# Weights of 64 bits cut to 32: raw words that land two bytes further, one cast and one join

## The chip, the cores and the metric

The kernel runs on one core of one Trainium2 chip. The metric is the device time of one execution in microseconds (us); smaller is better. The engines of the core are PE (TensorE: the matrix engine), DVE (VectorE), ACT (ScalarE), POOL (GpSimd) and SP (SyncE), which issues nearly all the DMAs.

## What is computed

Attention over 4 batches, 8 heads, 768 positions and 64 columns a head, in which a query sees the first n_global keys and the n_local keys up to itself, with a slope for each head; then two layers of two products each over 3072 tokens, with `h cos(h)` and `relu(h)` squared between them. q, k and v are 32-bit; the four weight matrices come in as 64-bit floats.

```python
def _moe_ref(x, w_in, w_out):            # 3072 x 512, 512 x 2048, 2048 x 512
    h = x @ w_in
    g = h * np.cos(h)
    return (g @ w_out).astype(np.float32)

def _moe2_ref(x, w_in, w_out):
    h = np.maximum(x @ w_in, 0.0)
    return (h * h @ w_out).astype(np.float32)

def reference(...):
    attn_out = _attn_ref(q, k, v, n_global, n_local)
    x = attn_out.transpose(0, 2, 1, 3).reshape(B * S, H * D)
    return _moe2_ref(x=_moe_ref(x=x, ...), ...)
```

## The kernel before

The 3072 tokens are cut into 24 tiles of 128 and six blocks of four tiles. Products run in 16-bit floats: each operand is split into a high half and what is left of it (a cast on ScalarE, then a subtraction on VectorE or GpSimd, `split_lo`, line 471, all recorded under line 474), and three products of halves are summed in PSUM. Only the attention of the first block (`group32`, line 762) runs in 32-bit products, since its operands then need no splitting. For each pair of heads and tile it goes: bias and scores on PE (lines 871 and 788), the maximum and its scaling on VectorE (lines 878 and 882), the exponential on ScalarE (line 886), a scaled unit matrix on VectorE (line 803), a transposing product (line 816), a copy (line 821), the product with the values (line 831), a copy into x (line 840). The other blocks' attention is `group` (line 891).

Weights come as 64-bit words. `decoded` (line 554) makes 32-bit floats of two tiles, 1024 words in each of 128 partitions: a DMA of 1024 KB (line 558) brings the raw words into a `raw` tile; ScalarE scales the upper words' absolute value, read as floats (`magnitude`, line 56); VectorE shifts it up by three bits (line 62), puts in the three top bits of the lower word (line 65), and puts in the sign (line 68), in place, in a `dec` tile. `weight` (line 566) then splits `dec` into 16-bit halves. The 16 decodes of the first layer lie at the beginning, up to the end of the first block's first layer; the 16 of the second layer come later (`seven_weights`, line 633, and `second_weights`, line 1551).

The instructions of the fast path are laid out by `Plan` (line 149). Each piece of work has an engine or several that may take it, an estimated duration, a due time, and the buffers that it reads and writes. The plan runs a model of the five engines, takes the ready piece with the earliest due time on each, gives out buffer slots, and writes the instructions down in the order found. Each engine executes its list in order. The `SHIFTS` table (line 84) moves the due times of groups of pieces: ('A', tile, pair) attention, ('P', tile) the loads and splits of a tile, ('W', e, unit) first-layer weights (e = 0: w_in, e = 1: w_out), ('X', tile) what follows a tile. The products of the two layers (`pe`, line 1110) keep the order in which they are written. Where the model finds PE idle before 240 us, filler matmuls on a tile of zeros are put in (line 1755).

Two raw slots, two dec slots and nine `ld` slots (used for keys, values and split weights) are shared by all. A DMA that waits for a slot stands at the head of SP's queue, with all later ones behind it. The slow, general path (line 1797) is not executed with these inputs.

Of the kernel before, what the change touches and what calls it, by code (L numbers as in the profile page):

```python
# [51 lines left out]
W_MAG = 2.0 ** -111  # L52


def magnitude(nc, t, r):
    nc.scalar.activation(out=t.bitcast(FP32), in_=r[:, :, 1].bitcast(FP32), func=ACTF.Abs, scale=W_MAG)


def join_steps(nc, t, r):

    return (
        lambda: nc.vector.tensor_scalar(  # L62
            out=t, in0=t, scalar1=3, scalar2=None, op0=ALU.logical_shift_left
        ),
        lambda: nc.vector.scalar_tensor_tensor(  # L65
            out=t, in0=r[:, :, 0], scalar=29, in1=t, op0=ALU.logical_shift_right, op1=ALU.bitwise_or
        ),
        lambda: nc.vector.scalar_tensor_tensor(  # L68
            out=t, in0=r[:, :, 1], scalar=-0x80000000, in1=t, op0=ALU.bitwise_and, op1=ALU.bitwise_or
        ),  # L70
    )

# [12 lines left out]
    ('A', 0, 0): 7.9,  # L85
    ('A', 0, 1): -2.2,
    ('A', 1, 0): -4.4,
    ('A', 1, 1): -2.2,
    ('A', 2, 0): -2.2,
    ('A', 2, 1): -2.2,  # L90
    ('A', 3, 0): -2.2,
    ('A', 3, 1): -2.2,
    ('A', 4, 0): -2.2,
    ('A', 4, 1): 4.2,
    ('A', 5, 0): -2.2,
    ('A', 5, 1): -19.1,
    ('A', 6, 0): -2.2,
    ('A', 6, 1): -2.2,
    ('A', 7, 0): -6.5,
    ('A', 7, 1): -8.6,  # L100
    ('A', 8, 0): -2.2,
    ('A', 8, 1): -2.2,
    ('A', 9, 0): -2.2,
    ('A', 9, 1): 1.7,
    ('P', 1): -1.8,
    ('P', 2): 7.8,
    ('P', 4): -21.4,
    ('P', 6): 9.8,
    ('P', 9): -13.4,
# [8 lines left out]
    ('W', 1, 0): -18.2,  # L118
    ('W', 1, 1): -12.2,
    ('W', 1, 2): -18.2,  # L120
    ('W', 1, 3): -13.1,
    ('W', 1, 4): -18.2,
    ('W', 1, 5): -12.7,
    ('W', 1, 6): -18.2,
    ('W', 1, 7): -24.7,
    ('X', 7): -17.9,
    ('X', 8): 3.7,
}
EARLY = 30.0
ROUNDS = 1  # L130
# [294 lines left out]
def fast_path(ctx, tc, kq, vt, w, n_raw, out, judge, ask):  # L425
# [39 lines left out]
    def new(pool):  # L465
        return Buf(pool)

    def lo_ways(n=512):
        return (("DVE", (n + 151) / 960, True), ("POOL", (n * 2.6 + 100) / 1200, True))
# [1327 lines left out]
def general_path(ctx, tc, kq, vt, w, raw, x_d, out):  # L1797
# [101 lines left out]
    def weights(m, e, j):  # L1899
# [4 lines left out]
        for f in join_steps(nc, t, r):  # L1904
            f()
# [102 lines left out]
```

## Time and profile before

| | us |
|---|---|
| median of 3 runs (lowest, highest) | 1084.62 (1083.74, 1085.63) |
| the profiled execution | 1085.72 |
| its span, first to last instruction | 1084.0 |
| PE busy | 1060.6 (98%) |
| DVE busy | 802.8 (74%) |
| ACT busy | 752.9 (69%) |
| POOL busy | 245.1 (23%) |

Busy times are those of the whole span; stages have different limits, so the rows below cut the span into stretches. The first matmul of the first layer begins at 61 us, and the last of its 16 first-layer weight pairs are decoded after 141 us. Matmuls are pipelined, and the ends of their records are modelled, so a busy PE need not be PE at its peak; filler matmuls count as busy.

### The profile page before, as it was taken

What the parts mean: (1) busy time and instruction counts of PE and PEld (TensorE: products, weight loads), DVE (VectorE), ACT (ScalarE), POOL (GpSimd) and SP (SyncE); (2) the same over time, 40 slices, a digit from 0 to 9 for tenths busy, and PEclk for the clock granted to TensorE, in tenths of its full rate; (3) what the DMA queues carried; (4) which work ended last, traced back from release to release, by engine and by line L of the source; (5) the groups of instructions that cost most, each with busy time, mean ns of one, the idle gap of its engine ahead of it and who ended that gap; (6) DMA issues with size and microseconds to landing.
All of it is one profiled execution on the core that took longest, in us unless ns stands there. A gap on an engine that the chain in (4) does not pass through costs nothing.

```text
span 1084.0 us, 23236 instructions
## 1 busy us (share of the span) xinstructions
PE 1060.6 (98%) x9380; PEld 753.3 (69%) x9380; DVE 802.8 (74%) x1483; ACT 752.9 (69%) x1349; POOL 245.1 (23%) x192
## 2 busy tenths in 40 slices
PE   6999999999999999999999999999999999999997
PEld 5754545554454444666666689888888888888887
DVE  7999997558688796677886687788368568477364
ACT  6999868998887674765876896555377457267361
POOL 1123320111140220233261221223024223033010
PEclk9999999999999999999999999999999999999999
DMA  6498888847867794778789897787564333334201
GB/s 234 171 243 250 238 282 246 152 97 238 229 177 209 295 338 157 246 226 229 249 272 261 233 232 222 268 315 255 195 216 135 127 137 127 128 117 156 86 4 41
DMA packets 160687, 217.69 MB, mean 201 GB/s; under 512 B 110464, under 2 KB 110976, under 8 KB 159040
## 3 DMA queue, kind: packets, MB, share of 16 engines
q1 hardware_dynamic: 160576, 216.17, 65.0%
q8 instruction: 74, 1.21, 0.5%
q14 instruction: 37, 0.30, 0.1%
HBM read 153.23 MB, written 36.70 MB: 175 GB/s over the span
## 4 chain that ended last, share of the span: by engine, by line
PE 83%; DVE 11%; ACT 4%; issue 1%; DMA 0%; DVEq 0%; SPq 0%; ACTq 0%
PE hps L1232 25%; PE ypps L1141 14%; PE hps L1125 13%; PE ypps L1368 11%; PE ypps L1438 7%; PE ypps L1183 7%; PE hps L922 2%; PE hps L983 2%; PE hps L1368 2%; DVE dec L65 1%; DVE nm L878 1%; DVE dec L68 1%; DVE dec L62 1%; DVE t L1426 1%; DVE xy L474 1%
## 5 line engine op out<-in xcount | busy, mean ns | idle before, releaser
L1232 PEld LDWEIGHTS <-ld 128*128 128x128 f16 x2400 | 234.0, 98 | 35.3 <-issue 2.6
L1232 PE MATMUL hps<-ys,ld 128*128 128x256 f16 x1680 | 195.1, 273 | 1.8 <-DVE t L1426 1.8
L1141 PE MATMUL ypps<-g,ld 128*128 128x512 f16 x768 | 177.8, 382 | 1.6 <-DVE g L474 1.6
L1125 PE MATMUL hps<-xy,w 128*128 128x512 f16 x768 | 174.5, 379 | 0.0
L1426 DVE TENSOR_TENSOR t<-hps,t 128x512 f32<-128x512 f32 x160 | 110.0, 688 | 66.4 <-PE hps L1232 64.3
L1141 PEld LDWEIGHTS <-ld 128*128 128x128 f16 x768 | 74.3, 98 | 90.2 <-issue 2.7
L1125 PEld LDWEIGHTS <-w 128*128 128x128 f16 x768 | 73.9, 98 | 86.2
L474 DVE TENSOR_TENSOR g<-t,g 128x512 f16<-128x512 f32 (+1 forms) x128 | 101.0, 793 | 26.0 <-ACT g L1209 25.2
L1209 ACT ACTIVATE g<-t 128x512 f16<-128x512 f32 x128 | 79.3, 622 | 23.5 <-DVE t L1165 21.8
L1183 PE MATMUL ypps<-g,ld 128*128 128x256 f16 x768 | 89.2, 273 | 0.5 <-DVE g L474 0.5
L1438 PE MATMUL ypps<-ld,g 128*128 128x512 f16 x384 | 89.5, 379 | 0.0
L1183 PEld LDWEIGHTS <-ld 128*128 128x128 f16 x768 | 75.0, 98 | 9.4 <-issue 0.6
L1423 ACT ACTIVATE t<-t 128x512 f32<-128x512 f32 x72 | 45.0, 624 | 48.9 <-DVE t L1426 48.6
L474 POOL TENSOR_TENSOR g<-t,g 128x512 f16<-128x512 f32 (+1 forms) x24 | 30.8, 1284 | 195.0 <-ACT g L1209 185.1
L1165 DVE SCALAR_TENSOR_TENSOR t<-t,hps 128x512 f32<-128x512 f32 x72 | 48.9, 682 | 31.9 <-ACT t L1163 31.9
L1161 ACT ACTIVATE t<-hps 128x512 f32<-128x512 f32 x72 | 42.7, 592 | 34.0 <-PE hps L1125 25.4
L1438 PEld LDWEIGHTS <-g 128*128 128x128 f16 x384 | 36.7, 98 | 37.1
L1163 ACT ACTIVATE t<-t 128x512 f32<-128x512 f32 x96 | 60.4, 629 | 2.6
L1258 ACT ACTIVATE t<-t 128x512 f32<-128x512 f32 x96 | 60.3, 628 | 2.5
L954 ACT ACTIVATE e<-e,nm 128x256 f32<-128x256 f32 (+1 forms) x128 | 52.7, 482 | 8.3 <-DVE nm L946 8.1
L946 DVE CUSTOM_DVE_ANT_0 e<-hps,bias 128x256 f32<-128x256 f32 (+2 forms) x128 | 43.2, 395 | 18.0 <-PE hps L922 17.9
L631 POOL TENSOR_TENSOR t<-t 128x256 f32<-128x256 f32 x18 | 16.4, 909 | 158.0 <-DVE x L631 157.9
(228 smaller groups left out, 1943.6 us busy)
## 6 DMA issues: line engine op xcount, KB each, us to landing
ld<-w SPq DMA_DIRECT2D x154, 512.0 KB, 4.3
raw<-w SPq DMA_DIRECT2D x32, 1024.0 KB, 6.6
w<-ld SPq DMA_DIRECT2D x44, 512.0 KB, 3.6
ld<-kq SPq DMA_DIRECT2D x23, 512.0 KB, 6.0
ld<-vt SPq DMA_DIRECT2D x24, 256.0 KB, 5.3
yd<-xy SPq DMA_DIRECT2D x6, 1024.0 KB, 5.8
xy<-yd SPq DMA_DIRECT2D x6, 1024.0 KB, 6.6
ld<-w SPq DMA_DIRECT2D x24, 256.0 KB, 4.0
```

The lines of the kernel that those rows point to most:

```text
L474: op.emit = lambda: eng[op.eng].tensor_tensor(out=out_f(), in0=src_f(), in1=hi_f(), op=ALU.subtract)
L954: nc.scalar.activation(out=at(e)[:, x, 0:W], in_=at(e)[:, x, 0:W], func=ACTF.Exp, bias=at(nm)[:, x:x + 1], scale=-1.0,)
L1125: nc.tensor.matmul(out=at(ps), lhsT=w_view(wt)[:, a, j % 2, k * 128:(k + 1) * 128], rhs=x_view(src)[:, c, k, :], start=(n == 0), stop=(n = ...
L1141: nc.tensor.matmul(out=at(y_ps[d]), lhsT=wv[:, a, d * 128:(d + 1) * 128], rhs=at(g)[:, c], start=(j == 0 and n == 0), stop=(j == NJ - 1 an ...
L1163: act(due + 1.2, 512, lambda: nc.scalar.activation(out=at(t), in_=at(t), func=ACTF.Square, scale=HALF_TURN), w=[t])
L1183: nc.tensor.matmul(out=at(y_ps[d])[:, 256 * n:256 * n + 256], lhsT=w_view(wt)[:, a, u, d * 128:(d + 1) * 128], rhs=at(g)[:, z, 256 * u:256 ...
L1209: act(due, 512, lambda: nc.scalar.activation(out=at(g)[:, 0], in_=at(t), func=ACTF.Copy), r=[t], new=[g])
L1232: nc.tensor.matmul(out=at(bank)[:, 256 * u:256 * u + 256], lhsT=wv(a, u, kk), rhs=sv(c, kk), start=(fresh and u == n == 0), stop=(last and ...
L1258: act(due, 512, lambda: nc.scalar.activation(out=at(t), in_=at(t), func=ACTF.Square), w=[t])
L1368: nc.tensor.matmul(out=at(bank)[:, 256 * half:256 * half + 256], lhsT=gv(home)[:, z, c0:c0 + 128], rhs=wv(a, u), start=(q == half == u == ...
L1426: dve(due, 0.7, lambda: nc.vector.tensor_tensor(out=at(t), in0=at(bank), in1=at(u), op=ALU.add), port=False, **k)
L1438: nc.tensor.matmul(out=at(y_ps[d]), lhsT=at(g)[:, z, 256 * u + d % 2 * 128:256 * u + d % 2 * 128 + 128], rhs=wv[:, a, u], start=(q == i == ...
```

## The change

A raw tile gets two more words a partition, and the DMA writes its data beginning two bytes into the row. A 32-bit word read at odd places then holds the upper half of the low word and the lower half of the high word, and shifted right by 13 it gives 19 bits of the wanted word. The topmost half-word of the 64-bit word, read as a bfloat16, is cast to float16 by ScalarE with a scale of 2, into the upper half of a word of a `top` tile whose lower halves were set to zero once. One VectorE instruction shifts and ors the two into a fresh `dec` tile. There is one `top` slot, and the cast's target is held until the join has read it.

Besides: in `group32` the scores come first and the bias is added after them, as a piece of its own; the scaling of the maximum is a piece of its own that VectorE, GpSimd or ScalarE may take; the bias tiles of the heads are built in another order, and two casts of the global tokens come after them; the cast of n stands later in `build_bias`; the 32-bit unit matrix is gone (the 16-bit one is read, and copied once near the end); the plan's model counts GpSimd's steps and the DMA rate otherwise and begins at 1.3 us; the `SHIFTS` are others.

```diff
-W_MAG = 2.0 ** -111
-def magnitude(nc, t, r):
-    nc.scalar.activation(out=t.bitcast(FP32), in_=r[:, :, 1].bitcast(FP32), func=ACTF.Abs, scale=W_MAG)
-def join_steps(nc, t, r):
-    return (
-        lambda: nc.vector.tensor_scalar(
-            out=t, in0=t, scalar1=3, scalar2=None, op0=ALU.logical_shift_left
-        ),
-        lambda: nc.vector.scalar_tensor_tensor(
-            out=t, in0=r[:, :, 0], scalar=29, in1=t, op0=ALU.logical_shift_right, op1=ALU.bitwise_or
-        ),
-        lambda: nc.vector.scalar_tensor_tensor(
-            out=t, in0=r[:, :, 1], scalar=-0x80000000, in1=t, op0=ALU.bitwise_and, op1=ALU.bitwise_or
-        ),
-    )
+UP = S_W ** 0.125
+def shifted(r, n):
+    return r.bitcast(INT16)[:, 1:4 * n + 1]
+def top_half(nc, t, r, n):
+    nc.scalar.activation(
+        out=t.bitcast(FP16).rearrange("p (c b) -> p c b", b=2)[:, :, 1],
+        in_=r.bitcast(BF16)[:, 4:4 * n + 4].rearrange("p (c b) -> p c b", b=4)[:, :, 0], func=ACTF.Copy, scale=UP)
+def join(nc, f, t, r, n):
+    nc.vector.scalar_tensor_tensor(
+        out=f, in0=r[:, 0:2 * n].rearrange("p (c b) -> p c b", b=2)[:, :, 1], scalar=13, in1=t,
+        op0=ALU.logical_shift_right, op1=ALU.bitwise_or)
...
 SHIFTS = {
-    ('A', 0, 0): 7.9,
-    ('A', 0, 1): -2.2,
-    ('A', 1, 0): -4.4,
+    ('A', 0, 0): -4.4,
+    ('A', 0, 1): 24.0,
+    ('A', 1, 0): -13.6,
...
-    ('P', 2): 7.8,
-    ('P', 4): -21.4,
+    ('P', 2): 33.0,
+    ('P', 4): -28.2,
...
-    ('W', 0, 0): -18.2,
-    ('W', 0, 1): -18.2,
-    ('W', 0, 2): -30.9,
-    ('W', 0, 3): -19.4,
-    ('W', 0, 4): -16.1,
-    ('W', 0, 5): -18.2,
-    ('W', 0, 6): -18.2,
-    ('W', 0, 7): -18.2,
+    ('W', 0, 0): 3.9,
+    ('W', 0, 1): -8.0,
+    ('W', 0, 2): -15.2,
+    ('W', 0, 3): -8.5,
+    ('W', 0, 4): -20.3,
+    ('W', 0, 5): -10.8,
+    ('W', 0, 6): -11.3,
+    ('W', 0, 7): -11.3,
...
+BEGIN = 1.3
+RATE = 320.0
...
-        raw=(2, [128, 1024, 2], INT32), ld=(9, [128, 1024], FP32), ...
+        top=(1, [128, 1024], INT32), raw=(2, [128, 2050], INT32), ld=(9, [128, 1024], FP32), ...
...
-        nc.vector.tensor_copy(out=ident32, in_=ident)
...
-        nc.vector.tensor_copy(out=nf, in_=n_raw[:, :, 0])
...
         nc.vector.tensor_tensor(out=t, in0=t, in1=rel, op=ALU.add)
+        nc.vector.tensor_copy(out=nf, in_=n_raw[:, :, 0])
...
+        nc.gpsimd.memset(slots["top"][0], 0)
...
     def decoded(m, e, jj, due):
-        t, raw = new("dec"), new("raw")
+        f, t, raw = new("dec"), new("top"), new("raw")
         dma(due - 12, 1024, lambda: nc.sync.dma_start(
-            out=r().rearrange("p (u a) b -> p u (a b)", u=2),
-            in_=w[m, e, 2 * jj:2 * jj + 2].bitcast(INT32).rearrange("u p c -> p u c")), new=[raw])
-        act(due - 7, 1140, lambda: magnitude(nc, at(t), r()), r=[raw], new=[t])
-        for n, us in enumerate((0.69, 1.22, 1.22)):
-            dve(due - 5.6 + 1.3 * n, us, lambda n=n: join_steps(nc, at(t), r())[n](), r=[raw] if n else [], w=[t])
+            out=shifted(at(raw), 1024).rearrange("p (u c) -> p u c", u=2),
+            in_=w[m, e, 2 * jj:2 * jj + 2].bitcast(INT16).rearrange("u p c -> p u c")), new=[raw])
+        act(due - 7, 1024, lambda: top_half(nc, at(t), at(raw), 1024), r=[raw], new=[t])
+        dve(due - 5.6, 1.22, lambda: join(nc, at(f), at(t), at(raw), 1024), r=[t, raw], new=[f])
...
-        plan.add((("PE", 2.0, False),), s, scores, r=reads, new=ps, lag=0.3, after=[biased[h] for h in heads])
+        k = dict(part=reads) if T == g == 0 else dict(r=reads)
+        plan.add((("PE", 1.3 if t else 0.65, False),), s, scores, new=ps, lag=0.3, **k)
+        plan.add((("PE", 0.65, False),), s + 0.5, lambda: add_bias(ps, g, adds, last=True), w=ps, lag=0.3,
+                 after=[biased[h] for h in heads])
         dve(s + 1, 1.4 * W / 256, lambda: largest(ps, nm, W), port=False, r=ps, new=[nm])
+        scaled(nm, s + 2.5)
...
+    def scaled(nm, due):
+        o = plan.add((("DVE", 0.17, True), ("POOL", 0.2, True), ("ACT", 0.21, False)), due, None, w=[nm])
...
-    dist_of = dve(0.0, 4.0, build_bias, r=[], after=())
-    for h in range(H):
-        biased.append(act(4.0 + PAIR * (h // 2), 320, lambda h=h: head_bias(h), after=[dist_of]))
+    dist_of = dve(0.0, 5.4, build_bias, r=[], after=())
+    biased = {}
+    for n, h in enumerate((0, 1, 4, 5, 2, 3, 6, 7)):
+        biased[h] = act(4.0 + PAIR * (n // 2), 215, lambda h=h: head_bias(h), after=[dist_of])
```

## Rows read from the trace of the kernel before

**Rows 1.** Stretches: bounds, length, PE, PEld, DVE, ACT, POOL busy, granted clock, DMA, GB/s.

```profile
0.00:20.00 20.00, 10.17 (x66) 7.53 (x67) 12.43 (x31) 12.60 (x32) 3.46 (x20) 1.00 0.85 302
20.00:61.00 41.00, 39.99 (x467) 30.60 (x467) 40.20 (x64) 37.70 (x93) 5.70 (x3) 1.00 0.53 160
61.00:141.00 80.00, 77.34 (x610) 39.22 (x609) 75.08 (x96) 71.61 (x114) 26.08 (x16) 0.99 0.87 247
141.00:161.00 20.00, 20.00 (x145) 9.38 (x145) 19.30 (x26) 11.35 (x18) 4.67 (x3) 0.94 0.79 274
161.00:1060.00 899.00, 894.74 (x7940) 650.35 (x7933) 647.85 (x1253) 617.38 (x1088) 205.17 (x153) 1.00 0.65 199
```

**Rows 2.** Stretches, instructions of line 1755 alone: length, PE and PEld busy, then as before.

```profile
20.00:61.00 41.00, 5.87 (x25) 2.21 (x25) 1.00 0.53 160
61.00:141.00 80.00, 2.06 (x8) 0.60 (x7) 0.99 0.87 247
```

**Rows 3.** Waits of PE over the span: us in total, times, longest us.

```profile
PE hps L871 <- ACT bias L523: 8.0, 2, 7.2
PE ypps L1141 <- DVE g L474: 1.6, 1, 1.6
```

**Rows 4.** Timeline of DVE and POOL near 133 us: start, us, instruction, idle time before.

```profile
133.48 3.15 DVE L65 SCALAR_TENSOR_TENSOR dec<-raw,dec 128x1024 int32<-128x1024 int32 x1
...
133.41 2.13 POOL L474 TENSOR_TENSOR ld<-dec,ld 128x1024 f16<-128x1024 f32 x1 [4.24 <-ACT ld L571]
```

**Rows 5.** The page's chain that ended last, share of the span by engine.

```profile
PE 83%; DVE 11%; ACT 4%; issue 1%; DMA 0%; DVEq 0%; SPq 0%; ACTq 0%
```

**Rows 6.** Instructions by source line: ns lowest/median/highest, first and last start, form.

```profile
L56 ACT ACTIVATE dec<-raw x32: 1125/1142/1220, 16.3 to 457.2; 128x1024 f32<-128x1024 f32 x32
...
L62 DVE TENSOR_SCALAR dec<-dec x32: 674/686/2089, 18.3 to 458.5; 128x1024 int32<-128x1024 int32 x32
...
L65 DVE SCALAR_TENSOR_TENSOR dec<-raw,dec x32: 1205/1224/3146, 19.1 to 464.9; 128x1024 int32<-128x1024 int32 x32
...
L68 DVE SCALAR_TENSOR_TENSOR dec<-raw,dec x32: 1211/1222/3153, 23.4 to 466.2; 128x1024 int32<-128x1024 int32 x32
...
L571 ACT ACTIVATE w<-dec x8: 1040/1044/1121, 27.4 to 138.9; 128x1024 f16<-128x1024 f32 x8
```

**Rows 7.** Stretches, DVE busy in line 62 (first two), line 68 (last two).

```profile
0.00:61.00 61.00, 3.43 (x5) 1.00 0.63 207
61.00:141.00 80.00, 8.54 (x9) 0.99 0.87 247
...
0.00:61.00 61.00, 6.09 (x5) 1.00 0.63 207
61.00:141.00 80.00, 10.98 (x9) 0.99 0.87 247
```

**Rows 8.** DMA issues: tiles, times, KB each, median us from issue to landing.

```profile
raw<-w SPq DMA_DIRECT2D x32, 1024.0 KB, 6.6
...
ld<-kq SPq DMA_DIRECT2D x2, 256.0 KB, 4.7
```

**Rows 9.** Waits of SP's queue from 0 to 145 us.

```profile
SPq L558 <- DVE dec L68: 41.3, 9, 10.7
```

**Rows 10.** Timeline of SP, DVE, ACT and PE in the first 12 us.

```profile
1.38 0.69 SPq L742 DMA_DIRECT2D ld<-kq  x1
...
3.51 0.17 DVE L504 CAST nf<-n_raw 128x2 f32<-128x2 int32 x1 [1.65 <-DMA n_raw<-n]
...
11.52 1.28 DVE L878 TENSOR_REDUCE nm<-hps 128x2 f32<-128x512 f32 x2
...
6.30 2.98 ACT L523 ACTIVATE bias<-dist 128x320 bf16<-128x320 f32 x8 [0.44 <-DVE dist L519]
...
9.13 0.80 PE L788 MATMUL hps<-ld 64*128 64x128 f32 x4
```

**Rows 11.** Timeline of PE near 61 us.

```profile
61.05 2.75 PE L1125 MATMUL hps<-xy,w 128*128 128x512 f16 x12
```

More of the change, by code (lines that the diff above doesn't have):

```diff
@@ L429, in fast_path @@
     kinds = dict(
[L430 removed]
+        top=(1, [128, 1024], INT32), raw=(2, [128, 2050], INT32), ld=(9, [128, 1024], FP32), ys=(4, [128, 2048], FP16), kq=(3, [128, 2, 2, HR, 128], FP16),
         v=(3, [128, H * (D + 1)], FP32), kg=(1, [128, 2, HR, GLOB], FP16), vg=(1, [GLOB, 2, H, D + 1], FP16),
@@ L485, in dve, with dma @@
         return plan.add((("DVE", us, port),), due, fn, **k)
-    def dma(due, kb, fn, issue=0.45, rate=300.0, **k):
+    def dma(due, kb, fn, issue=0.45, rate=RATE, **k):
         return plan.add((("SP", (issue, kb / rate), False),), due, fn, **k)
@@ L747, in prepare32 @@
             src = lambda: f4(f)[:, 0, :, 0:GLOB]
-            act(s + 30, 128, lambda: nc.scalar.activation(out=at(kg)[:, 0], in_=src(), func=ACTF.Copy), r=[f], new=[kg])
+            done = [biased[7]]
+            act(s + 30, 128, lambda: nc.scalar.activation(out=at(kg)[:, 0], in_=src(), func=ACTF.Copy), r=[f], new=[kg], after=done)
             dve(s + 31, 0.3, lambda: nc.vector.tensor_tensor(
@@ L753, in prepare32 @@
             act(s + 30, 512, lambda: nc.scalar.activation(
-                out=at(vg)[:, 0, :, 0:D], in_=hv(), func=ACTF.Copy, scale=S_V), r=[vf], new=[vg])
+                out=at(vg)[:, 0, :, 0:D], in_=hv(), func=ACTF.Copy, scale=S_V), r=[vf], new=[vg], after=done)
             dve(s + 31, 0.7, lambda: nc.vector.scalar_tensor_tensor(
@@ L872, in add_bias @@
                     out=p[:, :, c0:c1], lhsT=ident, rhs=bias[:, h0:h0 + 2, b0:b0 + c1 - c0],
-                    start=(n == 0), stop=False, skip_group_check=True,
+                    start=(n == 0 and not last), stop=last, skip_group_check=True,
                 )
@@ L1586, in farthest @@
             measured.append(last)
-        ps = new("h")
+        ps, unit = new("h"), new("t")
         def turned():
             for i in range(2):
-                nc.tensor.matmul(out=at(ps)[0:1, 128 * i:128 * i + 128], lhsT=longest[:, i:i + 1], rhs=ident32,
+                nc.tensor.matmul(out=at(ps)[0:1, 128 * i:128 * i + 128], lhsT=longest[:, i:i + 1], rhs=at(unit)[:, 0:128],
                                  start=True, stop=True)
-        plan.add((("PE", 0.5, False),), due + 1, turned, new=[ps], lag=0.3, after=measured)
+        dve(due, 0.3, lambda: nc.vector.tensor_copy(out=at(unit)[:, 0:128], in_=ident), new=[unit])
+        plan.add((("PE", 0.5, False),), due + 1, turned, r=[unit], new=[ps], lag=0.3, after=measured)
         def bound():
@@ L1730, in idle_products @@
                 continue
-            if last is not None and o.start < SPIN_UNTIL and biased[0].end < o.start:
+            if last is not None and o.start < SPIN_UNTIL and biased[7].end < o.start:
                 gap = o.start - last.end
@@ L1897, in general_path @@
                 )
+    top = gc.tile([128, 512], INT32, name="g_top")
+    vec.memset(top, 0)
     def weights(m, e, j):
-        r = gw.tile([128, 512, 2], INT32, tag="raw", name="g_raw")
-        nc.sync.dma_start(out=r.rearrange("p a b -> p (a b)"), in_=w[m, e, j].bitcast(INT32))
+        r = gw.tile([128, 1026], INT32, tag="raw", name="g_raw")
+        nc.sync.dma_start(out=shifted(r, 512), in_=w[m, e, j].bitcast(INT16))
         t = gw.tile([128, 512], INT32, tag="w", name="g_w")
-        magnitude(nc, t, r)
-        for f in join_steps(nc, t, r):
-            f()
+        top_half(nc, top, r, 512)
+        join(nc, t, top, r, 512)
         return t.bitcast(FP32)
```

98 lines of the change are left out of this document (53 added, 45 removed).

## Prediction

> **What bounds the kernel now.** I read three views in this order: busy time by stretch, what the matrix engine (PE) waits for, and the chain that ended last. The stretches [rows 1] show three regimes. From 161 to 1060 us PE is busy 894.74 of 899 us: nothing that makes another engine lighter can give more than the 4.3 us that are missing there. Between 20 and 61 us (attention of the first four tiles, 32-bit products) VectorE is the fullest engine, 40.20 of 41 us; PE shows 39.99, but 5.87 of that is filler matmuls of line 1755 that only keep it awake [rows 2], so its real work is 34.1 us. Between 61 and 141 us (first block of layer 1, while its weights are decoded) PE has 77.34 of 80 busy, 2.06 of it filler, VectorE 75.08, ScalarE 71.61: three engines near full together. The waits of PE agree [rows 3]: 8.0 us in two waits for the bias tiles at the very beginning, and 1.6 us for a VectorE result. That one is at 138 to 140 us [rows 4]: a join of line 65 met a GpSimd step that began at 133.41 us, took 3.15 us instead of 1.22, and the results PE needed stood behind it. After the stall the granted clock is 0.94 over 141 to 161 us [rows 1]: part of that stretch ran at 1.2 GHz instead of 2.4, worth 0.06 x 20 = 1.2 us. The chain puts 83% of the span on PE and 11% on VectorE [rows 5], and that 11% is the first 140 us.
>
> So the question is how much of PE's missing time before 161 us the change gives back. It is at most: 20 - 10.17 = 9.8 us in 0 to 20 us (most of it the loads' arrival), 41 - 34.1 = 6.9 in 20 to 61, 2.66 + 2.06 = 4.7 in 61 to 141, 1.2 after.
>
> **The change part by part.**
>
> *Decode.* Before, a pair of weight tiles costs one ScalarE pass (1.14 us) and three VectorE passes (0.69 + 1.22 + 1.22 = 3.13 us) [rows 6]. After, one ScalarE cast and one VectorE shift-and-or with the same two int32 inputs and the same strides as line 65, so 1.22 us. Removed from VectorE: 1.91 us for each of 32 decodes, 61 us in all, but 16 of them belong to layer 2, where PE is full: those give nothing. In the time that counts the lines that go (62 and 68) had 3.43 + 6.09 = 9.5 us before 61 us, and 8.54 + 10.98 = 19.5 us between 61 and 141 [rows 7]; line 62 there takes 0.95 us a time instead of 0.69, since it too meets GpSimd. VectorE therefore drops from 40.2 to about 31 of 41 us, and from 75 to about 56 of 80. It stops being the bound. What is next is ScalarE in 20 to 61 us (37.70 of 41) and PE itself, closely followed by ScalarE (71.61), in 61 to 141.
>
> *The ScalarE cast* reads half-words 8 bytes apart and writes half-words 4 bytes apart; the trace of before has no such pass. The nearest rows are line 56 (words 8 bytes apart, 1.14 us) and line 571 (dense words to half-words, 1.04) [rows 6]. I take 1.14, so ScalarE is unchanged; the other end is 0.1 us less for each of the 14 to 16 decodes before 161 us, some 1.5 us. A loss is not excluded if half-word writes with gaps are slower: at twice line 56, the nine decodes of 61 to 141 us would cost ScalarE 10 us, more than the 8.4 it has idle there. I keep that end for rival two. The Trainium skill (ScalarE: Activation LUTs, What ACT_TABLE_LOAD costs) gives an activation with immediate scale 186 ns + 0.833 ns an element for fp32 and bf16 alike, 1.04 us here as an estimate; line 56, at 1.14 us, shows that the stride is not free. By the page ScalarE would end 1.5 us lighter and the sum below at most 1 us lower.
>
> *The landing.* A raw tile of 1024 KB lands 6.6 us after its issue [rows 8] and DMA is busy 0.87 of 61 to 141 us at 247 GB/s [rows 1], 19.8 MB, of which the nine or ten raw tiles are about half (10 x 1.05 = 10.5 MB). What two bytes of offset cost no row shows. Lower bound 0; upper bound, each packet twice as long. I take 0 because the runs stay 4096 bytes long, and price the other end as a rival. The Trainium skill speaks against the change here (DMA: Bandwidth & Descriptors, How a descriptor splits into AXI transactions): a descriptor that does not begin on a 256-byte boundary takes one more transaction. For 4096 bytes that is 17 for 16, an estimate of 6%, and would move the share from 0.87 to 0.90, which changes no term; no run here shows it yet.
>
> *Buffers and the load queue.* A raw slot is freed by the single join instead of by the third pass, and the output slot is taken only at the join. SP's queue stood 41.3 us in nine waits of line 558 for line 68 [rows 9], with the later loads queued behind; these waits shrink. Against that, the cast's target "top" has one slot: the next cast waits for the last join, and ScalarE's later work stands behind it. A decode's turn is then about 1.14 + 1.22 us plus hand-overs, against one decode in about 9 us, so I cost it at nothing; the cover is gone when a join meets GpSimd (rival three).
>
> *The beginning.* PE's first products waited 7.2 us for the bias [rows 3], the first score products ran at 9.13, the first maximum began at 11.52 [rows 10]. Now scores go first and need only half of the first load (issued at 1.38 us; a 256 KB half takes 4.7 [rows 8], so 6.1 us); the bias tiles of the four heads of the first group come first of eight rather than among six (8 in 2.98 us, so 0.75 us less), and the cast that waits for n (3.51 us) stands two VectorE steps later, 0.8 us less. First group complete about 7.5 us, its maximum some 3.5 us earlier. Bounds 1 to 4; I take 3.0. The two global-token casts moved behind the eight bias tiles come back as two short casts on ScalarE, which is 7.4 us idle in 0 to 20 us. A bias product that waits at PE's head holds the next group's scores, as before. The zeroing of "top" falls to GpSimd, idle 16.5 of 20 us. All at nothing.
>
> *Shifts.* Of the first-layer weights, the w_in units come due later (seven of eight, by 7 to 22 us), the w_out units within 6 us of before, so fewer decodes press between 20 and 61 us. Tile 2's loads come due 25 us later, tile 4's 7 us earlier; all pass through one SP queue, in which a load that has no free slot holds those behind. I cost this inside the terms. The new scaling step (any of three engines), the unit-matrix copy near the end and the 16-bit unit matrix in line 803 are single short steps in stretches where VectorE now has room: nothing.
>
> **Sum**, against the profiled execution (1085.72 us, span 1084.0): beginning 3.0; 20 to 61 us 2.0 (between 0 and the 6.9 of PE; ScalarE allows 41 - 37.7 = 3.3, and hand-overs keep part); 61 to 141 us 2.7 of 4.7; the clock 1.2; after 161 us 0. Together 8.9, so 1076.8 us. The median of the runs is 1084.62, 1.1 lower than the profiled one, so 1075.7.
>
> **The rivals.**
>
> 1. *PE bound from the start.* All covers work: 4 + 6.9 + 4.7 + 1.2 and half of the 4.3 us after 161 us, 19 us: 1066. For it: VectorE's relief is far larger than the holes. Against: ScalarE at 37.7 of 41.
>
> 2. *ScalarE takes VectorE's place.* It loses nothing by the change and is 92% and 90% full. Then only the beginning and the clock are won, 4.2 us: 1080.4.
>
> 3. *The single slot and GpSimd.* A join that meets a GpSimd step takes 3.15 us; the next cast waits, and behind it on ScalarE the sine and the halves that PE needs. The stall at 138 us cost 1.6 us and 1.2 by the clock, 2.8 together. Three more like it cancel the gain, four or five make it slower: 1084 to 1088. Against: VectorE is no longer full, so there is less to stand behind.
>
> 4. *The landing at two bytes is slow (slower than before).* With raw tiles x longer, DMA's share of 61 to 141 us is 0.87 (1 + 0.53 x). It decides from x = 0.28 (share 1); from x = 0.45 the overrun eats the gain; with x = 1 the share is 1.33, 26 us over: 1105.
>
> **How the numbers follow.** Forecast (1071 to 1079.5) 0.53; rival one 0.13; two 0.16; three 0.11 (half unchanged, half slower); four 0.07. The range takes in rivals one and two and half of three: 1066 to 1085. A difference of 0.2% (2.2 us) is about what a measurement of this kernel can tell from none. Faster 0.82, within 0.2% 0.05, slower 0.13.
>
> **What would show it.** Right: VectorE about 31 of the stretch that now is 20 to 61 us, the first matmul of line 1125 some 5 us before 61.05 us [rows 11], fewer fillers, no clock below full after 30 us, the rest of the span as long as before. Wrong: raw tiles landing much later than 6.6 us, the cast over 1.2 us, waits of PE for ScalarE in the first block, or new waits after 161 us where I put zero.

## The result, and the profile after

| | before, us | after, us |
|---|---|---|
| median (lowest, highest) | 1084.18 (1083.63, 1085.63) | 1068.97 (1068.91, 1069.69) |
| the profiled execution | 1085.72 | 1068.98 |
| its span | 1084.0 | 1067.3 |

After over before is 0.9859, with an interval of 0.9842 to 0.9876: 15.2 us less, where 8.9 were forecast. The column of before is of the runs that shared the chip with after; its median is 0.4 us below the one that stands ahead of the prediction.

The stretches of the profile after, with the columns of [rows 1] (length, PE, PEld, DVE, ACT, POOL, granted clock, DMA share, GB/s), then the filler matmuls of two of them alone, which answer to [rows 2]:

```profile
0.00:20.00 20.00, 12.88 (x106) 10.14 (x107) 14.66 (x29) 14.21 (x44) 5.10 (x21) 1.00 0.88 328
20.00:61.00 41.00, 40.16 (x482) 30.80 (x482) 31.48 (x50) 40.75 (x97) 8.92 (x4) 1.00 0.66 189
61.00:141.00 80.00, 79.70 (x625) 40.00 (x624) 63.68 (x85) 76.94 (x122) 23.35 (x14) 1.00 0.88 265
141.00:161.00 20.00, 20.00 (x183) 11.12 (x181) 14.58 (x32) 19.23 (x29) 0.00 (x0) 1.00 0.92 274
161.00:1060.00 899.00, 897.47 (x7961) 657.31 (x7960) 615.21 (x1229) 612.43 (x1076) 185.23 (x137) 1.00 0.64 196
...
20.00:61.00 41.00, 2.98 (x13) 1.19 (x13) 1.00 0.66 189
61.00:141.00 80.00, 0.82 (x3) 0.21 (x3) 1.00 0.88 265
```

VectorE is no longer the full engine: 31.48 of 41 us instead of 40.20, 63.68 of 80 instead of 75.08. ScalarE is: 40.75 of 41 and 76.94 of 80. PE without its fillers does 37.18 us of work between 20 and 61 us (34.12 before) and 78.88 between 61 and 141 (75.28 before), and the granted clock is 1.00 from 20 us on, so the dip to 0.94 after 141 us is gone. VectorE would have been at about 56 of 80 us by the prediction. It is at 63.68 because 11 joins fall into that stretch instead of nine decodes, and because it now takes 11 of the subtractions for `g` there (9.2 us) instead of five (4.4), and five of those for the weights (8.0 us) instead of two (2.4).

What PE waits for over the span (us in total, times, longest), against [rows 3]; the page's chain that ended last, against [rows 5]; and three lines of the timeline, of PE, of VectorE and of PE again, against [rows 10, 11]:

```profile
PE hps L791 <- DMA ld<-kq: 5.4, 2, 4.5
PE hps L1250 <- DVE t L1444: 1.3, 1, 1.3
PE hps L890 <- ACT bias L530: 1.2, 2, 0.8
...
PE 92%; ACT 5%; DVE 2%; DMA 0%; issue 0%; SPq 0%; DVEq 0%; ACTq 0%
...
4.54 1.23 PE L791 MATMUL hps<-ld 64*128 64x128 f32 x8 [4.54 <-DMA ld<-kq]
...
6.99 0.42 DVE L897 TENSOR_REDUCE nm<-hps 128x2 f32<-128x256 f32 x1 [1.32 <-PE hps L890]
...
53.72 2.75 PE L1143 MATMUL hps<-xy,w 128*128 128x512 f16 x12
```

The bias tiles cost PE 1.2 us instead of 8.0; what it waits for first is now the load. In the chain the 11% of VectorE have become 2% and ScalarE has 5%. The first maximum begins 4.5 us earlier (6.99 against 11.52) and the first matmul of the first layer 7.3 us earlier (53.72 against 61.05).

The clock column says 1.00 for the first 20 us of both kernels, but the matmuls themselves say otherwise. The same product of 128x128 32-bit values (line 816, now 823), in before from 19 to 20.5 us and in after around 14 us (ns lowest/median/highest, first and last start):

```profile
L816 PE MATMUL ypps<-t,e x4: 411/421/580, 19.5 to 20.3; 128*128 128x128 f32 x4
```

```profile
L823 PE MATMUL ypps<-t,e x8: 275/275/420, 13.5 to 14.4; 128*128 128x128 f32 x8
```

In before these products begin 0.21 us apart until 20.5 us and 0.11 us apart from 20.7 us on, and last 275 ns then too. That is a factor of two, as between the two levels of the clock. So PE comes to its full speed some 7 us earlier in after, at 13.7 instead of 20.6 us. That is about what the first layer gains; how much of the gain is its doing, no run shows.

Since the products of the two layers have the same order in both kernels, the n-th matmul of a line can be set against the n-th of before. (Up to some 205 us attention products lie between them in other places, and the difference moves up and down by some us.) That gives the place of the gain: 7.3 us at the first matmul of the first layer, 12.5 from some 205 us of before on, 12.9 at 430 us, 16.6 at the end. I call 12.9 the early part and 3.7 the late part; every experiment below has the same two numbers, from its own profiled execution against that of before. That execution of before is 1.5 us above the median of 1084.18, so the two numbers add up to 1.4 us more than the 15.2 of the medians.

The decode, as [rows 6] had it (ns lowest/median/highest, first and last start, form), and the landing of the raw tiles, as [rows 8]:

```profile
L62 ACT ACTIVATE top<-raw x32: 1338/1352/1447, 19.9 to 425.1; 128x1024 f16<-128x1024 bf16 x32
L69 DVE SCALAR_TENSOR_TENSOR dec<-raw,top x32: 1206/1224/1261, 21.7 to 427.2; 128x1024 int32<-128x1024 int32 x32
...
raw<-w SPq DMA_DIRECT2D x32, 1024.0 KB, 6.1
```

The join costs 1.224 us as forecast, and GpSimd never holds it up: six of the 32 overlap a GpSimd step in time, but the longest takes 1.261. The cast costs 1.352 us; I took 1.14. The raw tiles land no later than before.

### The profile page after: what moved, and what is told of

Read it like the earlier page. It is cut to its first block, busy times and chain, and to the rows that moved or that the text cites. A ratio compares the mean times of both kernels' runs of the same rounds, so it can differ in the third digit from the quotient of the medians.

```text
span 1067.3 us, 23170 instructions
## 1 busy us (share of the span) xinstructions
PE 1052.0 (99%) x9364; PEld 750.8 (70%) x9364; DVE 741.9 (70%) x1426; ACT 763.6 (72%) x1363; POOL 222.6 (21%) x176
## 4 chain that ended last, share of the span: by engine, by line
PE 92%; ACT 5%; DVE 2%; DMA 0%; issue 0%; SPq 0%; DVEq 0%; ACTq 0%
PE hps L1250 27%; PE ypps L1159 15%; PE hps L1143 14%; PE ypps L1386 12%; PE ypps L1201 8%; PE ypps L1456 8%; PE hps L1002 2%; PE hps L940 2%; PE hps L1386 2%; ACT e L904 1%; ACT top L62 1%; PE hps L791 1%; ACT t L828 1%; DMA ld<-kq 0%; PE hps L1586 0%
## 5 line engine op out<-in xcount | busy, mean ns | idle before, releaser
L480 DVE TENSOR_TENSOR g<-t,g 128x512 f16<-128x512 f32 x131 | 98.6, 755 | 28.6 <-ACT g L1227 28.1
L1441 ACT ACTIVATE t<-t 128x512 f32<-128x512 f32 x72 | 45.0, 625 | 50.9 <-DVE t L1444 50.6
L480 POOL TENSOR_TENSOR g<-t,g 128x512 f16<-128x512 f32 (+1 forms) x21 | 27.9, 1329 | 120.8 <-ACT g L1227 109.7
L480 DVE TENSOR_TENSOR p<-e,p 128x1024 f16<-128x1024 f32 (+1 forms) x34 | 38.5, 1131 | 20.9 <-ACT p L989 20.8
```

Of the source, the lines that this page charges most:

```text
L480: op.emit = lambda: eng[op.eng].tensor_tensor(out=out_f(), in0=src_f(), in1=hi_f(), op=ALU.subtract)
```

## The experiments

Three theories stood against each other at first; the expectations call them A, B and C. A, that of the prediction: VectorE's relief is the gain, and the order of the work only passes it on. B: the relief makes room, and the new order (beginning, shifts, constants) collects it. C: the new order is the gain, and the decode comes along. Then the question was: is ScalarE, with a dearer cast, what now holds the early stretches, and does the landing cost anything?

**The new decode in the old order.** The kernel before, with the new `decoded`, its tiles and nothing else (the tile `dist` moves into a `ys` slot and the 32-bit unit matrix goes, as in the change, to make room).

```diff
-        act(due - 7, 1140, lambda: magnitude(nc, at(t), r()), r=[raw], new=[t])
-        for n, us in enumerate((0.69, 1.22, 1.22)):
-            dve(due - 5.6 + 1.3 * n, us, lambda n=n: join_steps(nc, at(t), r())[n](), r=[raw] if n else [], w=[t])
+        act(due - 7, 1024, lambda: top_half(nc, at(t), at(raw), 1024), r=[raw], new=[t])
+        dve(due - 5.6, 1.22, lambda: join(nc, at(f), at(t), at(raw), 1024), r=[t, raw], new=[f])
```

> The kernel before with the new decode alone (raw words two bytes further, one cast, one join; the top tile takes the place of the distance tile and of the 32-bit unit matrix, which move as in the change). Old due times, old beginning, old plan constants. Theory A (VectorE's relief is the source, worth most of the 15 us wherever the work is laid out): 1072 to 1077 us. Theory B (the relief only makes room; the due times and the beginning collect it): 1079 to 1083 us. Theory C (the decode brings nothing, all is beginning and due times): 1083 to 1086 us.

Measured: 1083.65 us, ratio 0.9993 (0.9983 to 1.0002). So VectorE's relief by itself is not the gain, although it is there (stretches, columns as above):

```profile
20.00:61.00 41.00, 39.70 (x477) 31.13 (x478) 32.90 (x55) 38.77 (x96) 6.22 (x3) 1.00 0.60 185
61.00:141.00 80.00, 78.93 (x614) 40.00 (x614) 64.71 (x91) 75.94 (x117) 16.55 (x8) 1.00 0.96 279
```

It isn't that nothing happened: early 5.1 us are gained, and late 4.6 are lost. What PE waits for over the span:

```profile
PE hps L864 <- ACT bias L520: 8.4, 2, 7.6
...
PE hps L1224 <- DVE t L1418: 2.2, 5, 0.9
PE ypps L1175 <- ACT g L1201: 2.0, 1, 2.0
```

The bias wait of the beginning stands as before (8.4 us), as it should. After 430 us there is a wait of 2.0 us for ScalarE that the kernel before has not; the last stretches will come back below.

**The old decode in the new order.** The kernel after, with the two replaced lines of the diff above put back, and with them the old landing and tiles.

> The changed kernel with the old decode put back (aligned landing, one ScalarE pass, three VectorE passes), new due times, new beginning, new constants. Theories A and B: VectorE is overfull again in the first 140 us, the new due times crowd the decodes later, so 1080 to 1092 us. Theory C: 1069 to 1073 us.

Measured: 1086.82 us, ratio 1.0023 (1.0013 to 1.0033): slower than before. In the profiled execution, early 4.2 us are lost and late 4.3 gained; it took 1085.64 us, 1.2 less than the median, and so shows less of the loss than the ratio does. So the order isn't the gain either: alone it is worth less than nothing. VectorE is what it runs into (stretch, and columns as above; first this kernel from 61 to 141 us, then what PE waited for in the first 161):

```profile
61.00:141.00 80.00, 76.04 (x584) 38.12 (x584) 75.92 (x83) 72.01 (x115) 36.97 (x20) 1.00 0.87 226
...
PE hps L1007 <- DVE t L1189: 1.9, 1, 1.9
PE ypps L828 <- DVE t L815: 1.5, 3, 0.6
PE ypps L1165 <- POOL ld L483: 1.2, 1, 1.2
```

**Old shifts; old beginning.** The kernel after with the whole `SHIFTS` table of before; and the new decode with the new shifts, but with the beginning and the constants of before.

```diff
 SHIFTS = {
-    ('A', 0, 0): -4.4,
+    ('A', 0, 0): 7.9,
...
```

> The changed kernel with the due times of before: new decode and new beginning. Theory A: 1069 to 1073 us. Theory B: 1075 to 1080 us, since weights are decoded as early as before, between 20 and 61 us, where ScalarE is next to full. Theory C: 1078 to 1083 us.

> The kernel before with the new decode and the new due times; beginning (bias ahead of scores, scaling in VectorE's hands, order of the bias tiles) and plan constants as before. The prediction put 3.0 us on the beginning: 1071 to 1074 us. If the new due times only fit the new beginning (tile 0's pairs are moved far apart), 1076 to 1082 us.

Measured: 1076.82 us (0.9930, 0.9913 to 0.9947) with the old shifts, early gain 5.2 and late 3.6; 1080.86 us (0.9961, 0.9947 to 0.9975) with the old beginning, early gain 8.8 and late loss 4.2. The second is not within the 1071 to 1074 us that the prediction's 3.0 us would make of it, but in the other range. So the new shifts add 3.7 us to the decode's 5.1, and the new beginning and constants some 4.1 to both. Without the shifts the beginning adds nothing (5.2 against 5.1). Each step pays only on top of the one before it. Of the three theories that leaves B: A's range for the decode alone (1072 to 1077) and C's for the old decode (1069 to 1073) are far off, while the old shifts land in B's range and the decode alone 0.7 us above it, in C's.

In the kernel with the old shifts one can see where the beginning's gain goes. Its first score product is 4.4 us earlier than in before, but the score products that before runs from 17.5 to 29 us come some 3.5 us later. Between them PE waits 2.3 us for the exponentials of the first group, and the granted clock falls to 0.84 over the first 20 us (after: 1.00). That stretch, with the columns of [rows 1], and that wait:

```profile
0.00:20.00 20.00, 11.70 (x60) 7.66 (x61) 12.30 (x25) 11.70 (x28) 2.77 (x20) 0.84 0.88 318
...
PE hps L784 <- ACT e L897: 2.3, 1, 2.3
```

**The two constants.** The late part goes with neither decode nor shifts: it is a gain in the three kernels so far that have the new constants (DMA rate 320, GpSimd's cost) and a loss in the two with the new decode and the old ones. So the kernel after, with those two numbers alone put back:

```diff
-RATE = 320.0
+RATE = 300.0
...
-        return (("DVE", (n + 151) / 960, True), ("POOL", (n * 2.3 + 200) / 1200, True))
+        return (("DVE", (n + 151) / 960, True), ("POOL", (n * 2.6 + 100) / 1200, True))
```

> The changed kernel with two plan constants of before: DMA rate 300 for 320, and GpSimd's step counted as (2.6 n + 100) cycles for (2.3 n + 200). In the runs so far the stretch after 430 us was 3.6 to 4.3 us shorter than before wherever the new constants and beginning were in (with either decode), and 4.2 to 4.6 longer with the new decode under the old ones. If these two constants lay out the late stretch: 1075 to 1079 us, the loss after 430 us. If the beginning's other edits do (the scaling as a piece of its own): 1068 to 1070.

Measured: 1076.01 us (0.9928), 7.0 slower than after: early gain 12.1 instead of 12.9, late loss 2.6 instead of a gain of 3.7. Late stretches, columns as above, first of before, then of after, then of this kernel:

```profile
430.00:630.00 200.00, 198.39 (x1906) 134.98 (x1904) 146.39 (x324) 148.75 (x275) 63.05 (x38) 1.00 0.83 241
630.00:800.00 170.00, 168.30 (x1661) 149.90 (x1659) 121.55 (x200) 100.45 (x178) 34.13 (x26) 1.00 0.77 248
```

```profile
430.00:630.00 200.00, 198.67 (x1989) 138.83 (x1983) 151.57 (x338) 151.97 (x283) 49.81 (x29) 1.00 0.90 250
630.00:800.00 170.00, 170.00 (x1612) 152.22 (x1609) 120.07 (x200) 99.12 (x176) 38.15 (x27) 1.00 0.72 241
```

```profile
430.00:630.00 200.00, 195.04 (x1881) 135.20 (x1881) 153.87 (x327) 149.36 (x277) 48.25 (x29) 1.00 0.89 247
630.00:800.00 170.00, 168.89 (x1671) 150.98 (x1666) 119.22 (x200) 99.55 (x177) 34.41 (x25) 1.00 0.74 244
```

PE idles 3.3 us in these 370 us before, 1.3 after, 6.1 with the old constants. The waits name what is late: after 430 us this kernel's PE waits 2.0 us once for ScalarE (line 1227), 1.8 for VectorE (line 1444) and 1.1 for a flag (line 1812); after waits 1.3 for line 1444 and for nothing else over 0.2. These numbers are in the plan's model alone and change no instruction, only which engine takes a step and in which order. Which of the two does it wasn't tried.

That 2.6 us are lost here, and 4.6 and 4.2 in the two kernels above, is a matter of the clock. All three have the same wait of 2.0 us for ScalarE. After it the granted clock falls in the decode alone (0.83 from 630 to 640 us) and in the kernel with the old beginning, and stays 1.00 here. The matmuls that follow the wait, in the decode alone and here:

```profile
633.58 4.18 PE L1175 MATMUL ypps<-g,ld 128*128 128x256 f16 x23 [0.54 <-DVE g L470]
```

```profile
625.91 2.67 PE L1201 MATMUL ypps<-g,ld 128*128 128x256 f16 x23 [0.54 <-DVE g L480]
```

The dip is worth 0.17 x 10 = 1.7 us, so without it the late loss under the old constants is 2.5 to 2.9 us in all three.

**The landing.** The kernel after with raw tiles that begin at the row's beginning; the cast reads the fourth half-word of each word, and the join the upper word.

```diff
-    return r.bitcast(INT16)[:, 1:4 * n + 1]
+    return r.bitcast(INT16)[:, 0:4 * n]
...
-        in_=r.bitcast(BF16)[:, 4:4 * n + 4].rearrange("p (c b) -> p c b", b=4)[:, :, 0], func=ACTF.Copy, scale=UP)
+        in_=r.bitcast(BF16)[:, 0:4 * n].rearrange("p (c b) -> p c b", b=4)[:, :, 3], func=ACTF.Copy, scale=UP)
```

> The changed kernel, raw words landing without the two bytes of offset; the cast reads the right half-word, the join reads the upper word instead of the one across, so the low bits of the weights are wrong; every instruction and its order are the same. If the offset landing costs nothing: within 0.1% of the changed kernel, 1068 to 1070 us, raw tiles landing in 6.0 to 6.2 us either way. If it costs one more transaction in seventeen: raw tiles about 0.2 us sooner, time the same. If it costs much and is hidden so far: raw tiles land in 4 to 5 us.

Measured: 1068.96 us against 1068.97, and every matmul within 0.5 us of its place in after. The raw tiles land in 6.4 us (after: 6.1), a cast takes 1.352 us as in after. Two bytes of offset cost nothing that can be seen. What this run can't show is a landing on a 256-byte boundary against one off it: in both programs the two raw tiles begin at bytes 5408 and 13632 of a partition, 32 and 64 past such a boundary. In before they begin at 1312 and 9504, each 32 past one.

**Joins twice, casts twice.** In each the instruction is issued twice in a row, with the plan told of one; the second writes the same again.

```diff
-        dve(due - 5.6, 1.22, lambda: join(nc, at(f), at(t), at(raw), 1024), r=[t, raw], new=[f])
+        dve(due - 5.6, 1.22, lambda: [join(nc, at(f), at(t), at(raw), 1024) for _ in range(2)], r=[t, raw], new=[f])
```

> The changed kernel, the join issued twice in each of 32 decodes (1.22 us of VectorE more each), order else the same, the plan unaware of it. If VectorE is no longer what limits the first 140 us: 0 to 3 us more, 1069 to 1072. If it still is: 16 x 1.22 = 20 us more at most, 1076 to 1089. VectorE would then do 2.44 us a decode, still under the 3.13 of before.

> The changed kernel, the cast issued twice in each decode (about 1.1 us of ScalarE more each), order else the same, the plan unaware of it. If ScalarE is the limit now from 20 to 161 us: 16 x 1.1 = 17 us more, 1080 to 1087, and more than the same surplus on VectorE costs. If PE alone is: 1069 to 1073.

Measured: 1086.16 us with two joins, 17.2 above after, and 1089.39 with two casts, 20.4 above after; nearly all of it before 300 and before 180 us. The first is in the range for a VectorE that still limits, the second 2.4 us above its own (1080 to 1087). The 16 early decodes have 16 x 1.22 = 19.6 us of second joins and 16 x 1.35 = 21.6 us of second casts. Joins in the first 161 us, after and with two joins, then casts in the kernel with two casts (us busy, times, granted clock):

```profile
0.00:161.00 161.00, 19.57 (x16) 1.00 0.83 255
0.00:161.00 161.00, 43.56 (x32) 0.99 0.77 237
...
0.00:161.00 161.00, 43.60 (x32) 0.98 0.74 222
```

The joins have become 24.0 us longer and not 19.6, since five of them overlap GpSimd steps and take 1.6 to 3.0 us. Matmul by matmul, the kernel with two joins has lost 12.4 us by 170 us and 3.8 more between 242 and 293 us; the one with two casts has lost all of its 20.3 by 170 us. So ScalarE passes on nearly everything that is laid on it, and VectorE about half, though VectorE shows 16.3 idle us between 61 and 141 us in after and ScalarE 3.1. Of these losses the clock has 0.04 x 41 = 1.6 us with two joins (granted 0.96 from 20 to 61 us) and 0.04 x 80 = 3.2 us with two casts (0.96 from 61 to 141 us). In the kernel with two joins, what ScalarE waited for in the first 161 us (its largest item), and in the kernel with two casts, what VectorE waited for:

```profile
ACT ld L576 <- DVE dec L69: 8.8, 6, 2.8
```

```profile
DVE dec L69 <- ACT top L62: 13.9, 9, 2.1
DVE t L1183 <- ACT t L1181: 8.9, 7, 2.3
```

ScalarE's next step of the same weight (its high half, line 576) stands at the head of its list and waits for the join, with the sines and copies that PE needs behind it. The idle time of VectorE isn't room: in a list that is carried out in order, an instruction that comes later holds whoever is written down behind its result.

**A cheaper cast.** The kernel after, with the cast on half of the columns.

```diff
-        act(due - 7, 1024, lambda: top_half(nc, at(t), at(raw), 1024), r=[raw], new=[t])
+        act(due - 7, 1024, lambda: top_half(nc, at(t)[:, 0:512], at(raw), 512), r=[raw], new=[t])
```

> The changed kernel, the cast done for half of the columns (0.43 us of ScalarE less a decode; the other half of the weights comes out as nearly zero), order the same. If ScalarE is the limit now: 3 to 7 us less, 1062 to 1066. If PE's own work and the loads are: 1067 to 1069.

Measured: 1066.87 us, 2.1 below after and between the two ranges. The cast takes 0.772 us instead of 1.352, so 16 x 0.58 = 9.3 us are taken off ScalarE, and between 61 and 141 us PE is then busy without a hole:

```profile
61.00:141.00 80.00, 80.00 (x628) 40.23 (x627) 63.30 (x93) 71.46 (x121) 22.86 (x14) 1.00 0.91 274
```

In that execution 1.7 us are won at the first matmul of the first layer already. So ScalarE is the next bound of the early part, but not far above PE itself: a load added to it costs nearly its whole length, a load taken away gives 2.1 of 9.3 us.

**Why the cast takes 1.35 us.** The kernel after, where even units cast from gapped half-words into dense ones, and odd units cast dense to gapped, dense to dense, and gapped to gapped as in after. Only the durations are of use here.

```diff
+            if jj % 2 == 0:
+                nc.scalar.activation(out=at(t).bitcast(FP16)[:, 0:1024], in_=words(), func=ACTF.Copy, scale=UP)
+            else:
+                nc.scalar.activation(out=gaps(), in_=dense(), func=ACTF.Copy, scale=UP)
+                nc.scalar.activation(out=at(t).bitcast(FP16)[:, 0:1024], in_=dense(), func=ACTF.Copy, scale=UP)
+                top_half(nc, at(t), at(raw), 1024)
```

> One look at the cast's own time by form, in the changed kernel: half of the decodes cast the same gapped half-words to a dense row; the other half do two more casts first, of a dense row of half-words to half-words with gaps, and to a dense row. The results of the weights are wrong in their low bits or altogether. The changed kernel's cast takes 1.352 us, the copies of dense words 1.044, the old pass over words 8 bytes apart 1.142. If the gaps of the writes cost: gapped to dense 1.04 to 1.14, dense to gapped about 1.25 to 1.35. If reading half-words 8 bytes apart costs: gapped to dense 1.35, dense to gapped 1.04. If both: 1.14 and 1.25. No claim on the whole time.

The four forms in that order (ns lowest/median/highest):

```profile
L573 ACT ACTIVATE top<-raw x16: 1108/1139/1230, 19.9 to 377.4; 128x1024 f16<-128x1024 bf16 x16
L575 ACT ACTIVATE top<-bias x16: 1337/1344/1407, 31.1 to 440.3; 128x1024 f16<-128x1024 bf16 x16
L576 ACT ACTIVATE top<-bias x16: 1056/1057/1057, 32.6 to 441.7; 128x1024 f16<-128x1024 bf16 x16
L62 ACT ACTIVATE top<-raw x16: 1352/1358/1375, 33.7 to 442.8; 128x1024 f16<-128x1024 bf16 x16
```

Dense takes 1.057 us; reading half-words 8 bytes apart adds 0.08; writing half-words 4 bytes apart adds 0.29, and hides most of the gapped read. My nearest row, line 56, has the gapped read but writes whole words: it could not show the dear half. My row of line 571 writes half-words, but dense ones.

**The cast on VectorE.** Since ScalarE is full and VectorE is not, the kernel after with the cast as a VectorE instruction, the plan told 1.22 us for it.

```diff
-        act(due - 7, 1024, lambda: top_half(nc, at(t), at(raw), 1024), r=[raw], new=[t])
+        op = plan.add((("DVE", 1.22, True),), due - 7, cast, r=[raw], new=[t])
```

> The changed kernel with the cast done by VectorE (a multiplication by 2, same half-words) in place of ScalarE, the plan told so: 1.35 us less of ScalarE, about 1.2 us more of VectorE a decode, 2.4 in all against 3.13 before. If ScalarE alone is what limits now (40.75 of 41 and 76.94 of 80 us busy): 1063 to 1067 us. If each engine is tied into the chain as tightly (the doubled join cost 17 us and the doubled cast 20): 1072 to 1085.

Measured: 1071.18 us (0.9880, 0.9863 to 0.9896), 2.2 above after and between the two ranges; the early gain is 10.8 instead of 12.9, the late one 3.6. Its two instructions, and its stretches from 20 to 141 us:

```profile
L571 DVE TENSOR_SCALAR top<-raw x32: 730/746/2416, 21.6 to 429.3; 128x1024 f16<-128x1024 bf16 x32
L69 DVE SCALAR_TENSOR_TENSOR dec<-raw,top x32: 1204/1220/3154, 22.4 to 431.9; 128x1024 int32<-128x1024 int32 x32
...
20.00:61.00 41.00, 39.85 (x471) 30.30 (x473) 34.70 (x53) 37.02 (x95) 9.84 (x4) 1.00 0.74 210
61.00:141.00 80.00, 78.03 (x632) 39.43 (x629) 73.70 (x98) 68.42 (x114) 37.10 (x18) 1.00 0.90 267
```

VectorE does the same cast in 0.746 us, and ScalarE gets lighter by 3.7 and 8.5 us in the two stretches. But GpSimd's steps between 61 and 141 us rise from 23.35 to 37.10 us, joins and casts meet them again (up to 3.154 and 2.416 us), and PE waits 2.0 us for one VectorE result (line 480) that it waits 0.2 us for in after. Those meetings are the ones that the prediction feared for the join in after, where none holds it up.

**The cast shared out.** As the last one, but 11 of the 16 first-layer casts and 5 of the later ones on VectorE, the plan told the measured 0.75 us, and a `SHIFTS` table fitted to that.

```diff
+        if (m, e, jj) in by_dve:
+            op = plan.add((("DVE", 0.75, True),), due - 7, cast, r=[raw], new=[t])
+        else:
+            op = act(due - 7, 1024, cast, r=[raw], new=[t])
```

> The kernel after, with half of the casts (11 of the 16 in the first layer, 5 of the 16 later ones) issued by VectorE and the plan told 0.75 us for these, which is what they took with all casts there, and with a SHIFTS table fitted to this. If ScalarE's load is what holds the early part above PE's own work, and VectorE has room for 11 x 0.75 = 8 us, the early gain against the kernel before goes from 12.9 to about 15 us, as with the cast on half the columns: about 1067 us, PE busy 80 of 80 between 61 and 141 us, ScalarE down by about 15 us (11 x 1.35) and VectorE up by 8. If instead every microsecond laid on a list that is carried out in order is passed on, wherever it stands, and joins and casts on VectorE meet GpSimd steps again (instructions of 2 to 3 us), it comes out no better than with all the casts on VectorE: 1070 to 1072 us. The late part stays at a gain of 3.6 in both.

Measured: 1071.22 us (0.9879, 0.9862 to 0.9895), 2.2 above after, as with all the casts on VectorE. The early gain is 10.7, the late 3.6. Its decode, and its stretch from 20 to 61 us:

```profile
L69 DVE SCALAR_TENSOR_TENSOR dec<-raw,top x32: 1211/1225/3149, 24.1 to 430.3; 128x1024 int32<-128x1024 int32 x32
L62 ACT ACTIVATE top<-raw x16: 1340/1350/1374, 22.7 to 380.2; 128x1024 f16<-128x1024 bf16 x16
L571 DVE TENSOR_SCALAR top<-raw x16: 734/748/2590, 26.4 to 429.5; 128x1024 f16<-128x1024 bf16 x16
...
20.00:61.00 41.00, 39.07 (x444) 29.81 (x443) 34.41 (x48) 36.42 (x91) 12.11 (x6) 0.96 0.70 206
```

Both engines have room now between 20 and 61 us (VectorE 34.41, ScalarE 36.42 of 41), and still the first matmul of the first layer comes 2.3 us later than in after, a lag that stays to the end. The granted clock is 0.96 in that stretch, which alone is 0.04 x 41 = 1.6 us, and a VectorE instruction that meets GpSimd takes up to 3.149 us. That a more even load would win was wrong in this order of work; how much of the 2.2 us is the clock's and how much the load's, no run separates. No version faster than after with all its work was found.

## Why the prediction was right, and where its sum was not

The direction was right, and so was the mechanism as far as it went: VectorE was the bound before 161 us, it stopped being so, and PE closed most of its holes. But the decode does not do this alone (0.9993); it needs the order, which the prediction had folded into its terms. The sum was 8.9 us and the runs give 15.2, so the time falls into the stated range (1066 to 1085) and out of the forecast's own (1071 to 1079.5): the range took in the rivals, and that made it wide enough. Its terms, one by one, in the profiled executions:

- *Beginning, 3.0 forecast.* The first maximum begins 4.5 us earlier. I had the first half of the load land at 1.38 + 4.7 = 6.1 us; PE's first product starts at 4.54, when it has landed. The 4.7 us were the median of two loads [rows 8], and it was no measure for the very first one, with nothing ahead of it. Undoing beginning and constants costs 4.1 us early (8.8 instead of 12.9); the two constants alone cost 0.8 (12.1), so 3.3 are left for the beginning, near the forecast. With it goes the scaling of the maximum, which I put at nothing: it cost VectorE 5.2 us from 20 to 141 us in before (line 882) and costs 0.7 in after (line 880). No run has it alone.
- *20 to 61 us, 2.0 forecast.* 7.3 us are won at the first matmul of the first layer, so 2.8 come on top of the first maximum's 4.5 (part of them perhaps before 20 us already, since PE comes to full speed 7 us earlier); PE's work in the stretch rises by 3.06 us and fillers fall from 5.87 to 2.98.
- *61 to 141 us, 2.7, and the clock, 1.2.* PE's work rises by 3.60, and the clock gives 1.2 (0.94 to 1.00 of 20 us): 4.8 by the rows, 5.2 by the places of the matmuls (12.5 - 7.3).
- *After 161 us, 0 forecast.* This is the step that failed: the matmuls show 0.4 us up to 430 and 3.7 after it. I read [rows 1] as leaving at most 4.3 us there, which held, but took none of it, since I took the constants of the plan for something that acts at the beginning. They order the whole program. Under the old ones the new decode makes the late part 2.6 us worse (4.6 and 4.2 with a dip of the clock), under the new ones it is 3.7 better, so the two numbers move it by 6.3 us.
- *Shifts, costed inside the terms.* They give 3.7 us early on top of the decode. The decode's own terms (2.0 + 2.7 + 1.2 = 5.9) stand against 5.1 measured alone, which is near; I had let the decode stand for the whole of the early gain, and the shifts add to it.
- *The cast, 1.14.* It takes 1.352, outside the bounds of the sum (1.04 to 1.14), because neither of the nearest rows writes half-words with gaps. The prediction had named such a loss and kept it for rival two, at twice line 56 (2.28 us), which was far too much. The Trainium skill (ScalarE: Activation LUTs, What ACT_TABLE_LOAD costs) gave 1.04 as an estimate: it fits the dense form (1.057) and misses the gapped write by 0.3. What this cost is bounded by the cheaper cast: 2.1 us.
- *The join, 1.22, and the single slot.* 1.224, and the next cast waited for a join once, 1.7 us. SP's queue stands 18.5 us in six waits for the join instead of 41.3 in nine [rows 9], as forecast, but other waits take their place: all its waits from 0 to 145 us are 104 us in both kernels.

```profile
SPq L564 <- DVE dec L69: 18.5, 6, 6.5
```

- *The landing, 0.* Right: 1068.96 against 1068.97 us without the offset. The rule of the Trainium skill that the prediction set against the change (DMA: Bandwidth & Descriptors, How a descriptor splits into AXI transactions), 6% more as an estimate, is about a start off a 256-byte boundary. No run here tests it: the raw tiles lie off such a boundary in before, in after and without the offset (6.6, 6.1 and 6.4 us to land), so by that rule the change would have cost nothing either.

The measured time lies between the forecast's own range (from 1071) and rival one (1066), nearer to the second in kind: PE idles 0.30 us between 61 and 161 us, and 1.53 us between 161 and 1060 where [rows 1] had 4.3. What rival one left out of account is the 2.98 us of fillers that remain, all from 50.9 us on, right before the first layer. Rival two was half right: ScalarE did take VectorE's place (40.75 of 41, and a doubled cast costs nearly its whole length), but it stands only 2.1 us above PE's own work, so the early gain was 12.9 us instead of 4.2. Rival three did not come: no join is longer than 1.261 us. Its long joins do come when VectorE is given the casts as well. Rival four is ruled out by the run without the offset.

Of the signs that I named, VectorE at 31.48 of 41 us (though 63.68 of 80 in the next stretch, where I had 56), the first layer 7.3 us earlier (some 5 were named), fewer fillers and a full clock came as told; the cast over 1.2 us, named as a sign against, came too, and the rest of the span was not as long as before.

What stays open: which of the two constants arranges the late part, and why the early gains of shifts and beginning need each other (the beginning alone gives nothing over the decode's 5.1). For the second, the wait for ScalarE and the dip of the clock in the first 20 us show where the gain is lost, but which of the old shifts brings them about, no run separates.

## What to carry to other kernels

A change of one instruction and the order around it are one change: here the instruction alone gave nothing (0.9993), the order alone lost (1.0023), and together they gave 15 us, so a part is judged only in an order made for it. Idle time of an engine in a fixed order is not room; doubling a step on an engine that idled 16 of 80 us still cost about half of what the engine then did more. And a number that a planner uses is a change to every stage that it plans, so its price can't be put at zero for the stages that the diff doesn't seem to touch.

## What was not expected of the hardware

- A ScalarE cast of 128 x 1024 half-words takes 1.057 us dense to dense, 1.139 when it reads 8 bytes apart, 1.344 when it writes 4 bytes apart, 1.35 with both.
- VectorE does the same cast with both gaps in 0.746 us, but up to 2.590 when it meets GpSimd.
- A landing two bytes further along the row made no difference: 1024 KB in 6.1 us, and 6.4 without the offset; neither lies on a 256-byte boundary.
- The clock column does not show that PE begins slow: the same product took 421 ns up to 20.5 us in before and 275 ns after it, in after 275 ns from 13.7 us on.
